# One head per numerator matmul: 64x64 tiles of TensorE in an attention-and-GLU kernel

## The chip, the cores and the metric

The kernel runs on one core of one Trainium2 chip. The metric is the device time of one execution in microseconds (us); where several executions were timed, their median. The changed kernel is compared with the kernel before on the same inputs.

## The reference, cut to what matters

Four batches of 1088 tokens, four heads of 32 numbers. Each query and key is mapped to 64 features (an outer product of two projections to 8), attention is linear in these features, and the result goes through a gated feed-forward layer (GLU) of width 1536.

```python
q_p, k_p = phi(q), phi(k)                       # [b, h, s, 64]
kv  = einsum('bhsf,bhsd->bhfd', k_p, v)         # 64 x 32 for each batch and head
z   = sum(k_p, over s)                          # 64 for each batch and head
num = einsum('bhsf,bhfd->bhsd', q_p, kv)        # the numerators
den = einsum('bhsf,bhf->bhs', q_p, z) + 1e-6
x   = num / den                                 # [b, s, h*32] = 4352 tokens x 128
xn  = x / sqrt(mean(x*x) + 1e-6) * rms_g
out = (silu(xn @ w_gate) * (xn @ w_val)) @ w_out
```

## The kernel before, in words

**Chunks.** The 4352 query tokens are worked in nine chunks: eight of 512 tokens and a last one of 256. `kside(b)` builds, for each batch, the table `kv` (key features times values, with a column of ones beside the values, so that numerator and denominator come out of one matmul). `qside(c)` builds the query features `phiq` of a chunk, then numerators, division, normalization and the two rounded halves `x_hi` and `x_lo` of the layer's input. `slot(c, j, t)` is one of the 12 blocks of 128 columns of the GLU for one chunk: three matmul passes each into `g_ps` and `v_ps` (L788) and three into `o_ps` (L826). These are called dense passes here.

**Small matmuls.** Beside the dense passes, TensorE runs fp32 matmuls on parts of the array. The trace shows each of them as two MATMUL records with a weight load (LDWEIGHTS) before each, so 16 matmuls of the program are 32 records. The forms that matter (rows of the array by columns of the array, as the trace writes them): L505 and L580 128*64 (projections of the first batch and of the first two chunks), L517 (`kvmm`: `kv`) 128*64 in batch 0 and 128*32 in the others, L483 and L608 64*32 (projections), L664 (`nmm`: the numerators) 128*64 in chunks 0 and 1 and 128*32 from chunk 2 on. L588 and L744 are transposes with the whole array.

**The numerators.** Heads are held in pairs `p`: `phiq[:, p, :]` has the 64 features of one head in partitions 0 to 63 and of the other in 64 to 127, and `kv[:, p, :]` is block-diagonal, so that a matmul over 128 rows gives both heads in 66 columns; half of what it multiplies is zeros. From chunk 2 (`spread`, L646) a matmul takes 32 tokens; a task `nmm` covers two blocks of 128 tokens with 16 matmuls and writes one PSUM bank (`att`, of which there are three, `ATT`). Behind it: `den` (add epsilon; ACT or DVE), `rden` (reciprocal, DVE), `x` (multiply, DVE, L672), two `mean` (L695, DVE), then for the chunk `rstd` (POOL, L707), `xn` (DVE or ACT), and from chunk 2 on a turn through DRAM (`xq`, `turned`, `xt`).

**What sets the order.** Each piece of work is a task of a planner (`Plan`). `ORDER` is a list of task numbers written into the file, `ON` a string that says on which engine a task runs that may run on several. Every engine executes its tasks in the order of that list; the planner's own costs (`pe(490, ...)` and the like) only place warm-up matmuls. DMAs of weights, keys, values and queries stand in the same list, on SP's queue.

**Instruction counts.** All dense passes count one MATMUL record each. The 2238 records of TensorE come in the order that the list sets.

Of the kernel before, what the change touches and what calls it, by code (L numbers as in the profile page):

```python
# [86 lines left out]
"""  # L87
ON = (
    "dapapadaddaadaadddaaaaapapdapapaadaadaadaapaadaadaadaadaddaadppddaapaadaaddadadadadadadadpdddaadddaaapapadadapapaadapapd"
    "dapapadapadapdpddddpadaaddadaapadaddpddadddadapadapddddadpadaadapaddpadapadddapapddadaaadpdaadpadadapddadddddapdpddddddd"  # L90
    "ddaaaapapapddapapdpdpddadaddpadadddaaaddddpapddadaddpadddapaddaddddaaddddpddapadadapadaddddpadpadddadadadadddapdda"
# [195 lines left out]
def attention_then_glu(ctx, tc, kT, v, qT, sw, w, out):  # L287
# [13 lines left out]
    def gate(i):  # L301
        return ps(("g_ps", "v_ps")[i], 2)
# [255 lines left out]
    def qside(c):  # L558
# [86 lines left out]
        x, xn = sb("x", [P, 4, H, D], 2), sb("xn", [P, 4 * DM], 2)  # L645
# [3 lines left out]

        def scaled_of(lo, hi):  # L650
            return xn()[:, :nt * DM].rearrange("p (h t d) -> p t h d" if spread else "p (t h d) -> p t h d", h=H, t=nt)[:, lo:hi]

        for u in range(0, nt, 2):
            num = gate(u // 2 if NUM_GATE < 2 else 1) if c <= NUM_GATE else ps("att", ATT)
            den, rden = sb("den", [P, 8, 1], 2), sb("rden", [P, 8, 1], 2)
            wide = D if spread else HALF

            def nmm(u=u, num=num, wide=wide):
                nv = num()[:, :4 * 66].rearrange("p (t a x) -> p t a x", t=2, a=2)
                for t in range(2):  # L660
                    for p in range(2):
                        for n0 in range(0, P, wide):
                            l0 = n0 // D * g + (u + t) * D if spread else (u + t) * P + n0
                            nc.tensor.matmul(  # L664
                                out=nv[n0:n0 + wide, t, p, :], lhsT=phi()[:, p, l0:l0 + wide], rhs=kvs[(s0 + l0) // S][:, p, :], start=True, stop=True,
                            )

            def view(num=num):
                return num()[:, :4 * 66].rearrange("p (y x) -> p y x", x=D + 1)

            def divide(u=u, view=view, rden=rden):
                nc.vector.tensor_tensor(  # L672
                    out=x()[:, u:u + 2], in0=view()[:, :, :D].rearrange("p (t h) d -> p t h d", t=2),
                    in1=rden().rearrange("p (t h) o -> p t h o", t=2).to_broadcast([P, 2, H, D]), op=ALU.mult,
                )
# [259 lines left out]
```

## Time and profile before

| | |
|---|---|
| median of 3 runs | 253.28 us (252.86, 253.28, 255.46) |
| the profiled execution: its time, its span | 252.8 us, 250.6 us |
| TensorE busy | 245.6 us, 98% of the span |
| VectorE, ScalarE, GpSimd busy | 180.4, 132.9, 82.1 us (72, 53, 33%) |
| chain that ended last, share of TensorE | 96% |
| first dense pass starts; last one starts | 16.18 us; 246.44 us |

The span is the profiled execution from its first to its last instruction; the time of that execution is 2.2 us longer. A busy TensorE is not at its peak: records of small matmuls lie over one another, so starts, not durations, tell how fast they pass.

### The profile page before, as it was taken

How to read it: one execution, taken by the hardware profiler on the slowest of the kernel's cores; microseconds unless marked ns; L12 is line 12 of the kernel's file. 1: busy time of each engine (PE TensorE's matmuls, PEld its weight loads, DVE VectorE, ACT ScalarE, POOL GpSimd, SP SyncE). 2: the span in 40 equal slices, each digit the busy share in tenths (PEclk: the TensorE clock that was granted, in tenths of full speed). 3: DMA queues.
4: the chain of work that ended last, by engine and by line, in shares of the span. 5: the costliest groups of instructions: out<-in, count | busy, mean ns of one | idle time of the engine just before them, and what ended most of it. 6: DMA issues, size and time to landing. Idle time of an engine off the chain costs nothing.

```text
span 250.6 us, 5851 instructions
## 1 busy us (share of the span) xinstructions
PE 245.6 (98%) x2238; PEld 197.8 (79%) x2238; DVE 180.4 (72%) x410; ACT 132.9 (53%) x287; POOL 82.1 (33%) x80
## 2 busy tenths in 40 slices
PE   7999999998999999999999999999999999999995
PEld 4977788776888788888888788888888888888894
DVE  1999989798367887675587678855678576765672
ACT  3696987574344747353445643553356464355351
POOL 4547130442663223223450403265332203132201
PEclk9999999999999999999999999999999999999999
DMA  6989992642372332421610352250003001010010
GB/s 235 368 274 347 271 244 77 166 143 44 74 213 67 85 83 94 105 86 32 163 55 1 60 165 86 42 177 35 3 0 63 24 3 42 28 56 3 0 43 21
DMA packets 18539, 25.55 MB, mean 102 GB/s; under 512 B 3024, under 2 KB 9296, under 8 KB 18512
## 3 DMA queue, kind: packets, MB, share of 16 engines
q1 hardware_dynamic: 18080, 24.54, 33.3%
q10 hardware_dynamic: 432, 0.66, 0.7%
q8 instruction: 17, 0.28, 0.5%
q14 instruction: 10, 0.08, 0.1%
HBM read 20.40 MB, written 4.78 MB: 100 GB/s over the span
## 4 chain that ended last, share of the span: by engine, by line
PE 96%; DMA 1%; issue 0%; SPq 0%; DVE 0%
PE v_ps L788 29%; PE g_ps L788 29%; PE o_ps L826 28%; PE att L664 3%; PE att L517 2%; DMA q<-qT 1%; PE att L608 1%; PE o_ps L517 1%; PE att L744 1%; PE att L483 1%; PE g_ps L664 0%; PE att L588 0%; PE v_ps L664 0%; PE att L580 0%; PE att L807 0%
## 5 line engine op out<-in xcount | busy, mean ns | idle before, releaser
L797 ACT ACTIVATE s<-g_ps 128x512 f32<-128x512 f32 (+1 forms) x108 | 61.1, 574 | 71.4 <-PE g_ps L788 38.5
L800 DVE TENSOR_TENSOR h<-v_ps,s 128x512 f32<-128x512 f32 (+2 forms) x110 | 69.7, 646 | 40.0 <-PE v_ps L788 27.6
L818 POOL TENSOR_TENSOR h_lo<-h,h_hi 128x512 fp32r<-128x512 f32 (+1 forms) x42 | 53.0, 1269 | 105.0 <-DVE h_lo L818 43.8
L339 ACT CAST h_hi<-h 128x512 fp32r<-128x512 f32 (+1 forms) x70 | 41.3, 601 | 19.9 <-DVE h L800 17.5
L818 DVE TENSOR_TENSOR h_lo<-h,h_hi 128x512 fp32r<-128x512 f32 (+1 forms) x64 | 41.3, 651 | 5.5 <-ACT h_hi L339 3.6
L788 PE MATMUL v_ps<-x_hi,w_hi 128*128 128x512 f32 (+1 forms) x110 | 41.9, 381 | 0.0
L788 PE MATMUL g_ps<-x_hi,w_hi 128*128 128x512 f32 (+1 forms) x110 | 41.8, 380 | 0.0
L788 PE MATMUL v_ps<-x_hi,w_lo 128*128 128x512 f32 (+1 forms) x110 | 41.6, 378 | 0.0
L788 PE MATMUL g_ps<-x_hi,w_lo 128*128 128x512 f32 (+1 forms) x110 | 41.6, 378 | 0.0
L788 PE MATMUL g_ps<-x_lo,w_hi 128*128 128x512 f32 (+1 forms) x110 | 41.5, 378 | 0.0
L788 PE MATMUL v_ps<-x_lo,w_hi 128*128 128x512 f32 (+1 forms) x110 | 41.3, 378 | 0.0
L826 PE MATMUL o_ps<-h_hi,w_hi 128*128 128x512 f32 (+1 forms) x106 | 40.9, 386 | 0.0
L826 PE MATMUL o_ps<-h_hi,w_lo 128*128 128x512 f32 (+1 forms) x106 | 40.8, 385 | 0.0
L826 PE MATMUL o_ps<-h_lo,w_hi 128*128 128x512 f32 (+1 forms) x106 | 40.8, 385 | 0.0
L788 PEld LDWEIGHTS v_ps<-x_hi,w_hi 128*128 128x128 f32 x110 | 20.6, 188 | 5.0 <-DVE w_lo L422 0.5
L788 PEld LDWEIGHTS g_ps<-x_hi,w_hi 128*128 128x128 f32 x110 | 20.7, 188 | 4.5
L788 PEld LDWEIGHTS v_ps<-x_hi,w_lo 128*128 128x128 f32 x110 | 20.7, 188 | 4.3
L788 PEld LDWEIGHTS g_ps<-x_hi,w_lo 128*128 128x128 f32 x110 | 20.7, 188 | 4.2
L788 PEld LDWEIGHTS g_ps<-x_lo,w_hi 128*128 128x128 f32 x110 | 20.6, 188 | 4.1
L788 PEld LDWEIGHTS v_ps<-x_lo,w_hi 128*128 128x128 f32 x110 | 20.5, 188 | 4.2
L826 PEld LDWEIGHTS o_ps<-h_lo,w_hi 128*128 128x128 f32 x106 | 19.9, 188 | 4.3
L826 PEld LDWEIGHTS o_ps<-h_hi,w_hi 128*128 128x128 f32 x106 | 19.9, 188 | 4.2
(110 smaller groups left out, 245.0 us busy)
## 6 DMA issues: line engine op xcount, KB each, us to landing
w_raw<-w SPq DMA_DIRECT2D x12, 384.0 KB
bt<-far SPq DMA_DIRECT2D x24, 128.0 KB
at<-far SPq DMA_DIRECT2D x12, 256.0 KB
outT<-o_sb SPq DMA_DIRECT2D x8, 256.0 KB
q<-qT SPq DMA_DIRECT2D x7, 256.0 KB
turned<-xq SPq DMA_DIRECT2D x24, 64.0 KB
xt<-turned SPq DMA_DIRECT2D x6, 256.0 KB
vt<-v SPq DMA_DIRECT2D x4, 272.0 KB
```

The source lines that it names most:

```text
L339: "act": on_act(n, lambda: nc.scalar.copy(out=out(), in_=in_()), True),
L483: nc.tensor.matmul(out=pair[p]()[a * D:(a + 1) * D, :g], lhsT=sblk[p * HALF:(p + 1) * HALF, p * NB // 2:(p + 1) * NB // 2], rhs=kt()[p * H ...
L517: nc.tensor.matmul(out=kvv[r0:r0 + wide, h // 2, :], lhsT=phi()[:, t, h * F + f:h * F + f + wide], rhs=vt()[:, t, h, :], start=(t == 0 and ...
L608: nc.tensor.matmul(out=accs[p]()[a * D:(a + 1) * D, :m], lhsT=sab[rows, p].rearrange("p c o r -> p (c o r)"), rhs=q()[rows, a * m:(a + 1) ...
L664: nc.tensor.matmul(out=nv[n0:n0 + wide, t, p, :], lhsT=phi()[:, p, l0:l0 + wide], rhs=kvs[(s0 + l0) // S][:, p, :], start=True, stop=True,)
L744: nc.tensor.transpose(out=xt()[:, t * P:(t + 1) * P], in_=xn()[:, t * DM:(t + 1) * DM], identity=ident)
L788: nc.tensor.matmul(out=acc()[:, cs], lhsT=wt[:, j, i3, :], rhs=x()[:, cs], start=(i == 0), stop=(i == 2))
L797: act(n, lambda: nc.scalar.activation(out=s()[:, :n], in_=gps()[:, :n], func=AF.Silu), cols(gps, whole[0]), [s])
L800: cs.stop - cs.start, lambda cs=cs: nc.vector.tensor_tensor(out=h()[:, cs], in0=vps()[:, cs], in1=s()[:, cs], op=ALU.mult),
L818: eng.tensor_tensor(out=h_lo()[:, :n], in0=h()[:, :n], in1=h_hi().bitcast(F32)[:, :n], op=ALU.subtract)
L826: nc.tensor.matmul(out=o_ps()[:, :n], lhsT=wt[:, j, 2, :], rhs=x()[:, :n], start=first and i == 0, stop=last and i == 2,)
```

## The change

From chunk 2 on, one numerator task covers the whole chunk. A matmul takes one head: 64 rows (that head's features), 64 tokens as columns of the array, and 33 moving columns instead of 66. The heads in partitions 0 to 63 write one bank, those in 64 to 127 a second. A full chunk has 32 such matmuls, as many as the two tasks before had together. Denominators, reciprocals and divisions are taken for each bank (two of each in a full chunk, as before; in the last chunk of 256 tokens two where one was), and all means of a chunk wait for both divisions. `x` is laid out head by head as `xn` was. Tokens of a chunk stay in natural order through `nmm`; the 32x32 transposes later leave them permuted, which the host undoes on the output's rows. `ORDER` and `ON` are new throughout. The core of the diff:

```diff
-            wide = D if spread else HALF
-            def nmm(u=u, num=num, wide=wide):
...
-                for t in range(2):
-                    for p in range(2):
-                        for n0 in range(0, P, wide):
-                            l0 = n0 // D * g + (u + t) * D if spread else (u + t) * P + n0
-                            nc.tensor.matmul(
-                                out=nv[n0:n0 + wide, t, p, :], lhsT=phi()[:, p, l0:l0 + wide], rhs=kvs[(s0 + l0) // S][:, p, :], start=True, stop=True,
...
-            pe(490, 8 * P // wide, nmm, of + [...], [num], None, 32 if spread else 64)
+        if spread:
+            nums = [ps("att", ATT) for _ in range(2)]
+            def nmm():
+                for t in range(nt):
                     for p in range(2):
+                        for hh in range(2):
+                            rows = slice(hh * F, (hh + 1) * F)
+                            for n0 in range(0, P, HALF):
+                                l0, y = t * P + n0, p * nt + t
+                                nc.tensor.matmul(
+                                    out=nums[hh]()[n0:n0 + HALF, y * (D + 1):(y + 1) * (D + 1)], lhsT=phi()[rows, p, l0:l0 + HALF],
+                                    rhs=kvs[(s0 + l0) // S][rows, p, hh * (D + 1):(hh + 1) * (D + 1)], start=True, stop=True,
+                                )
+            pe(122 * nt + 15, 16 * nt, nmm, [(phi, "p", p) for p in range(2)] + batches(0, n), nums, None, 33)
+            for hh in range(2):
...
+                rden = denominators(nums[hh], view, 2 * nt)
...
+                dve(64 * nt, divide, [nums[hh], rden], [(x, hh)])
+            made_of = {t: [(x, 0), (x, 1)] for t in range(nt)}
...
+        rows = o[s0:s0 + n]
+        res[s0:s0 + n] = rows.reshape(4, n // P, D, DM).transpose(1, 0, 2, 3).reshape(n, DM) if c >= XT else rows
```

How the new list moves TensorE's instructions is shown at three places. A row is one kind of instruction: line, output and inputs (with running numbers), output partitions x columns, and how often it comes in a row.

TensorE before, from the projection of a chunk (L608) over the `kv` products of batch 2 (L517) to the two numerator tasks of chunk 3:

```order
L608 MATMUL att_1107<-q_949,sab 32x128 x4
L608 MATMUL att_1112<-q_949,sab 32x128 x4
L517 MATMUL att_1118<-vt_589,phi_987 32x34 x72
L664 MATMUL att_1204<-kv_75,phiq_1105 32x66 x16
L664 MATMUL att_1228<-kv_75,phiq_1105 32x66 x16
```

The same products of batch 2 in the change, with L483 (keys' projection) ahead and one numerator task behind (here L682; 16 rows like the last two, in alternation):

```order
L483 MATMUL att_1119<-kt_984,sblk 32x288 x4
L483 MATMUL att_1124<-kt_984,sblk 32x288 x4
L517 MATMUL att_1131<-vt_580,phi_931 32x34 x72
L682 MATMUL att_1215<-kv_75,phiq_1103 64x33 x2
L682 MATMUL att_1218<-kv_75,phiq_1103 64x33 x2
```

L517 and the numerators had the same form of 128*32 and now have different ones; the projection of queries (L608), which stood in this group, now stands alone among dense passes. Over the whole program, from the first dense pass on, the small fp32 matmuls stood in 9 places among the dense passes and now stand in 12; the three numerator tasks that stood last in one place of 48 matmuls (chunks 7 and 8) now stand in two places, of 32 and 16.

TensorE before, around the first numerators of the program (L664 on 128*64, chunk 0):

```order
L517 MATMUL o_ps_210<-vt_114,phi_142 64x34
L517 MATMUL att_211<-vt_114,phi_142 64x34
L588 MATMUL att_262<-ident,at_217 128x128 x4
L664 MATMUL g_ps_271<-kv_73,phiq_208 64x66 x8
L664 MATMUL v_ps_284<-kv_73,phiq_208 64x66 x8
L588 MATMUL att_298<-ident,at_217 128x128 x4
```

And now (L713 are these numerators):

```order
L517 MATMUL o_ps_178<-vt_112,phi_143 64x34
L517 MATMUL att_179<-vt_112,phi_143 64x34
L580 MATMUL att_244<-sblk,q_127 64x64 x4
L580 MATMUL att_250<-sblk,q_127 64x64 x4
L713 MATMUL g_ps_259<-kv_73,phiq_215 64x66 x8
L713 MATMUL v_ps_274<-kv_73,phiq_215 64x66 x8
L588 MATMUL att_290<-ident,at_272 128x128 x4
```

Chunk 1's projection (L580) has come to stand right before the first numerators, and four of its transposes (L588) have gone behind them.

TensorE before, where the dense passes (L788) begin, with the transposes of chunk 0's x (L744) ahead and a warm-up matmul (L369) between them:

```order
L744 MATMUL att_402<-ident,xn_359 128x128 x2
L369 MATMUL att_409<-const-float32-0.0 1x128
L744 MATMUL att_417<-ident,xn_359 128x128 x2
L788 MATMUL v_ps_422<-x_hi_413,w_hi 128x256
L788 MATMUL v_ps_422<-x_hi_413,w_lo 128x256
```

And now (L786 are the transposes, L830 the dense passes):

```order
L786 MATMUL att_377<-ident,xn_352 128x128 x2
L483 MATMUL g_ps_385<-kt_154,sblk 32x288 x4
L483 MATMUL v_ps_390<-kt_154,sblk 32x288 x4
L608 MATMUL att_406<-q_270,sab 32x128 x4
L608 MATMUL att_411<-q_270,sab 32x128 x4
L830 MATMUL g_ps_418<-x_hi_398,w_hi 128x256
L830 MATMUL g_ps_418<-x_hi_398,w_lo 128x256
L786 MATMUL att_427<-ident,xn_352 128x128 x2
L830 MATMUL v_ps_434<-x_hi_398,w_hi 128x256
```

The second pair of transposes now comes after two dense passes, and two projections stand between the first pair and these passes.

## Rows read from the trace of the kernel before

**Rows 1.** By stretch: its length, PE, PEld, DVE, ACT, POOL busy, clock, DMA, GB/s.

```profile
0.00:16.20 16.20, 14.79 (x289) 10.81 (x289) 10.47 (x36) 9.87 (x32) 8.54 (x21) 1.00 0.83 295
62.00:64.00 2.00, 1.60 (x95) 1.50 (x95) 1.04 (x3) 0.72 (x2) 1.20 (x1) 1.00 0.10 22
64.00:120.00 56.00, 56.00 (x526) 44.93 (x526) 39.54 (x87) 28.19 (x56) 19.54 (x17) 1.00 0.34 93
176.00:246.70 70.70, 70.70 (x356) 59.29 (x355) 48.09 (x107) 33.67 (x71) 16.64 (x14) 1.00 0.09 23
```

**Rows 2.** The chain that ended last: start, length, what. A run of dense passes.

```profile
101.99 3.50 PE o_ps L826 x15
```

**Rows 3.** PE's timeline: start, duration, instruction, count. Chunk 2's numerators alone.

```profile
44.51 0.39 PE L788 MATMUL g_ps<-x_lo,w_hi 128*128 128x512 f32 x1
44.83 1.14 PE L664 MATMUL att<-kv,phiq 128*32 128x66 f32 x64
45.90 0.50 PE L826 MATMUL o_ps<-h_hi,w_hi 128*128 128x512 f32 x1
46.23 0.39 PE L826 MATMUL o_ps<-h_hi,w_lo 128*128 128x512 f32 x1
```

**Rows 4.** PE's timeline: a query projection, then numerators.

```profile
83.19 0.39 PE L826 MATMUL o_ps<-h_lo,w_hi 128*128 128x512 f32 x1
83.51 0.45 PE L608 MATMUL att<-q,sab 64*32 64x128 f32 x16
83.89 1.17 PE L664 MATMUL att<-kv,phiq 128*32 128x66 f32 x64
84.98 0.50 PE L788 MATMUL g_ps<-x_hi,w_hi 128*128 128x512 f32 x1
```

**Rows 5.** PE's timeline: projection, kv products and numerators in one place.

```profile
112.80 0.39 PE L788 MATMUL v_ps<-x_lo,w_hi 128*128 128x512 f32 x1
113.50 1.00 PE L517 MATMUL att<-vt,phi 128*32 128x34 f32 x94
114.31 0.23 PE L664 MATMUL att<-kv,phiq 128*32 128x66 f32 x1
115.79 0.51 PE L788 MATMUL v_ps<-x_hi,w_hi 128*128 128x512 f32 x1
```

**Rows 6.** PE's timeline: the same instructions 53 us earlier, with an idle time.

```profile
59.89 0.39 PE L788 MATMUL v_ps<-x_lo,w_hi 128*128 128x512 f32 x1
62.40 0.42 PE L517 MATMUL att<-vt,phi 128*32 128x34 f32 x28 [0.63 <-issue]
63.74 0.49 PE L788 MATMUL g_ps<-x_hi,w_hi 128*128 128x512 f32 x1
```

**Rows 7.** PE's timeline: 128*64 products of batch 0, 34 moving columns.

```profile
8.37 0.22 PE L517 MATMUL o_ps<-vt,phi 128*64 128x34 f32 x1
...
8.49 0.22 PE L517 MATMUL o_ps<-vt,phi 128*64 128x34 f32 x1
```

**Rows 8.** PE's timeline: 128*64 numerators of chunk 0, 66 moving columns.

```profile
11.04 0.69 PE L664 MATMUL g_ps<-kv,phiq 128*64 128x66 f32 x16
11.56 0.64 PE L664 MATMUL v_ps<-kv,phiq 128*64 128x66 f32 x16
12.13 0.33 PE L588 MATMUL att<-ident,at 128*128 128x128 f32 x1
```

**Rows 9.** Weight loads by form: busy us, mean ns | idle before.

```profile
L664 PEld LDWEIGHTS att<-kv,phiq 128*32 128x32 f32 x416 | 6.4, 110 | 1.0 <-issue 0.9
L517 PEld LDWEIGHTS o_ps<-vt,phi 128*64 128x64 f32 x36 | 2.2, 138 | 0.2 <-POOL phi L438 0.2
L608 PEld LDWEIGHTS att<-q,sab 64*32 64x32 f32 x112 | 1.3, 104 | 2.1 <-issue 1.6 <-PE o_ps L826 0.4
```

**Rows 10.** Timelines of PE and ACT at the start.

```profile
10.46 0.66 PE L588 MATMUL att<-ident,at 128*128 128x128 f32 x4
16.18 0.39 PE L788 MATMUL v_ps<-x_hi,w_hi 128*128 128x256 f32 x1
15.07 0.69 ACT L717 ACTIVATE xn<-x,rstd 128x128 f32<-128x128 f32 x2
```

More of the change, by code (lines that the diff above doesn't have):

```diff
@@ L648, in qside, with tokens, x_of @@
         xs[c] = (x_hi, x_lo)
+        def tokens(t, lo, hi):
+            return t()[:, :nt * DM].rearrange("p (h t d) -> p t h d" if spread else "p (t h d) -> p t h d", h=H, t=nt)[:, lo:hi]
+        def x_of(lo, hi):
+            return tokens(x, lo, hi)
         def scaled_of(lo, hi):
-            return xn()[:, :nt * DM].rearrange("p (h t d) -> p t h d" if spread else "p (t h d) -> p t h d", h=H, t=nt)[:, lo:hi]
-        for u in range(0, nt, 2):
-            num = gate(u // 2 if NUM_GATE < 2 else 1) if c <= NUM_GATE else ps("att", ATT)
+            return tokens(xn, lo, hi)
@@ L655, in qside, with batches, denominators @@
+        def batches(lo, hi):
+            return [("kv", b, i) for b in sorted({(s0 + lo) // S, (s0 + hi - 1) // S}) for i in range(2)]
+        def denominators(num, view, wide):
             den, rden = sb("den", [P, 8, 1], 2), sb("rden", [P, 8, 1], 2)
-            wide = D if spread else HALF
-            def nmm(u=u, num=num, wide=wide):
-                nv = num()[:, :4 * 66].rearrange("p (t a x) -> p t a x", t=2, a=2)
-                for t in range(2):
-                    for p in range(2):
-                        for n0 in range(0, P, wide):
-                            l0 = n0 // D * g + (u + t) * D if spread else (u + t) * P + n0
-                            nc.tensor.matmul(
-                                out=nv[n0:n0 + wide, t, p, :], lhsT=phi()[:, p, l0:l0 + wide], rhs=kvs[(s0 + l0) // S][:, p, :], start=True, stop=True,
-                            )
@@ L668, in view @@
[L668 to L674, printed above, removed]
-                )
-            if spread:
-                bs = {(s0 + a * g + (u + t) * D) // S for a in range(4) for t in range(2)}
-            else:
-                bs = {(s0 + (u * P)) // S, (s0 + (u + 2) * P - 1) // S}
@@ L681, in qside @@
-            of = [(phi, u)] if c < NATURAL else [(phi, "p", p) for p in range(2)]
-            pe(490, 8 * P // wide, nmm, of + [("kv", b, i) for b in sorted(bs) for i in range(2)], [num], None, 32 if spread else 64)
-            plan.add({
-                "dve": on_dve(20, lambda view=view, den=den: nc.vector.tensor_scalar_add(den(), view()[:, :, D:D + 1], EPS)),
-                "act": on_act(20, lambda view=view, den=den: nc.scalar.activation(
-                    out=den(), in_=view()[:, :, D:D + 1], func=AF.Copy, bias=EPS), against=DEN_ACT),
-            }, [num], [den])
@@ L688, in qside @@
-            dve(45, lambda den=den, rden=rden: nc.vector.reciprocal(out=rden(), in_=den()), [den], [rden])
-            dve(256, divide, [num, rden], [(x, u)])
-            for t in range(2):
-                sq = sb("sq", [P, DM], 2)
-                def mean(t=t, u=u, sq=sq):
-                    one = x()[:, u + t]
-                    nc.vector.tensor_tensor_reduce(
-                        out=sq().rearrange("p (h d) -> p h d", h=H), in0=one, in1=one, scale=1.0 / DM, scalar=EPS, op0=ALU.mult, op1=ALU.add,
-                        accum_out=ms()[:, u + t:u + t + 1],
-                    )
-                plan.add({"dve": Way(265, 345, mean, True)}, [(x, u)], [sq, (ms, u + t)])
+            plan.add({
+                "dve": on_dve(20, lambda: nc.vector.tensor_scalar_add(den()[:, :wide], view()[:, :, D:D + 1], EPS)),
+                "act": on_act(20, lambda: nc.scalar.activation(
+                    out=den()[:, :wide], in_=view()[:, :, D:D + 1], func=AF.Copy, bias=EPS), against=DEN_ACT),
+            }, [num], [den])
@@ new lines, in denominators, with view, divide, nmm @@
+            dve(45, lambda: nc.vector.reciprocal(out=rden()[:, :wide], in_=den()[:, :wide]), [den], [rden])
+            return rden
+        if spread:
+            nums = [ps("att", ATT) for _ in range(2)]
+            def nmm():
+                for t in range(nt):
+                    for p in range(2):
+                        for hh in range(2):
[8 more added lines that the diff above has]
+            for hh in range(2):
+                def view(hh=hh):
+                    return nums[hh]()[:, :2 * nt * (D + 1)].rearrange("p (y x) -> p y x", x=D + 1)
+                rden = denominators(nums[hh], view, 2 * nt)
+                def divide(hh=hh, view=view, rden=rden):
+                    nc.vector.tensor_tensor(
+                        out=x()[:, :nt * DM].rearrange("p (a r t d) -> p r a t d", a=2, r=2, t=nt)[:, hh],
+                        in0=view()[:, :, :D].rearrange("p (a t) d -> p a t d", a=2),
+                        in1=rden()[:, :2 * nt].rearrange("p (a t) o -> p a t o", a=2).to_broadcast([P, 2, nt, D]), op=ALU.mult,
+                    )
+                dve(64 * nt, divide, [nums[hh], rden], [(x, hh)])
+            made_of = {t: [(x, 0), (x, 1)] for t in range(nt)}
+        else:
+            for u in range(0, nt, 2):
+                num = gate(u // 2 if NUM_GATE < 2 else 1) if c <= NUM_GATE else ps("att", ATT)
+                def nmm(u=u, num=num):
+                    nv = num()[:, :4 * 66].rearrange("p (t a x) -> p t a x", t=2, a=2)
+                    for t in range(2):
+                        for p in range(2):
+                            for n0 in range(0, P, HALF):
+                                l0 = (u + t) * P + n0
+                                nc.tensor.matmul(
+                                    out=nv[n0:n0 + HALF, t, p, :], lhsT=phi()[:, p, l0:l0 + HALF], rhs=kvs[(s0 + l0) // S][:, p, :],
+                                    start=True, stop=True,
+                                )
+                def view(num=num):
+                    return num()[:, :4 * 66].rearrange("p (y x) -> p y x", x=D + 1)
+                pe(490, 16, nmm, [(phi, u)] + batches(u * P, (u + 2) * P), [num], None, 64)
+                rden = denominators(num, view, 8)
+                def divide(u=u, view=view, rden=rden):
+                    nc.vector.tensor_tensor(
+                        out=x_of(u, u + 2), in0=view()[:, :, :D].rearrange("p (t h) d -> p t h d", t=2),
+                        in1=rden().rearrange("p (t h) o -> p t h o", t=2).to_broadcast([P, 2, H, D]), op=ALU.mult,
+                    )
+                dve(256, divide, [num, rden], [(x, u)])
+            made_of = {t: [(x, t // 2 * 2)] for t in range(nt)}
@@ L702, in qside, with mean @@
+        for t in range(nt):
+            sq = sb("sq", [P, DM], 2)
+            def mean(t=t, sq=sq):
+                one = x_of(t, t + 1)[:, 0]
+                nc.vector.tensor_tensor_reduce(
+                    out=sq().rearrange("p (h d) -> p h d", h=H), in0=one, in1=one, scale=1.0 / DM, scalar=EPS, op0=ALU.mult, op1=ALU.add,
+                    accum_out=ms()[:, t:t + 1],
+                )
+            plan.add({"dve": Way(265, 345, mean, True)}, made_of[t], [sq, (ms, t)])
         for u, wd in ((0, 2), (2, 2)) if first else ((0, nt),):
@@ L703, in qside @@
             us, cs = slice(u, u + wd), slice(u * P, (u + wd) * P)
-            ids = list(range(u, u + wd, 2))
+            ids = sorted({k for t in range(u, u + wd) for k in made_of[t]}, key=lambda k: k[1])
             def root(us=us):
@@ L710, in scaled @@
                 nc.vector.tensor_tensor(
[L711 removed]
+                    out=scaled_of(u, u + wd), in0=x_of(u, u + wd),
                     in1=rstd()[:, u:u + wd].unsqueeze(3).to_broadcast([P, wd, H, D]), op=ALU.mult,
@@ L722, in qside @@
                 "act": Way(wd * 300 + 5, wd * 300 + 85, scaled_act, against=SCALED_ACT),
-            }, [(x, i) for i in ids] + [(rstd, u)], [(xn, u)])
+            }, ids + [(rstd, u)], [(xn, u)])
             if spread:
@@ L933 @@
     r = run_bass_kernel_spmd(nc, [arrays], core_ids=[0])
-    return np.ascontiguousarray(r.results[0]["outT"].T)
+    o = r.results[0]["outT"].T
+    res = np.empty((NT, DM), np.float32)
+    for c, (s0, n) in enumerate(zip(STARTS, CHUNKS)):
+        rows = o[s0:s0 + n]
+        res[s0:s0 + n] = rows.reshape(4, n // P, D, DM).transpose(1, 0, 2, 3).reshape(n, DM) if c >= XT else rows
+    return res
```

11 lines of the change are left out of this document (5 added, 6 removed), and 70 rows, old and new, of the table ORDER.

## The prediction

> **What bounds the kernel now.** I read the busy time by stretch first. TensorE is busy for 56.00 of 56.00 us and for 70.70 of 70.70 us in the stretches after 64 us, while the next busiest engine, DVE, has 39.54 and 48.09 [rows 1]. So TensorE is the bound, and the kernel's end moves by what its instruction stream gains or loses. The chain of waits then tells what a dense pass costs: 15 passes of 512 columns in 3.50 us, so 0.233 us each [rows 2]. Before and after each group of small matmuls the timeline gives the rest: from the start of the last dense pass before the group to the start of the second one after it, less two passes of 0.233, is what the group costs. The chunk's numerators alone cost 46.23 - 44.51 - 0.47 = 1.25 us [rows 3]. Only the start (up to 16.18 us [rows 10]) and a hole near 62 us, where TensorE is busy for 1.60 of 2.00 us [rows 1], are not full.
>
> The sum below is made against the profiled execution, 252.8 us with a span of 250.6; it lies 0.5 under the median of the three runs, 253.28, and nothing in the change touches the 2.2 us outside the span.
>
> **The numerators themselves.** A full chunk keeps its 32 matmuls, hence 64 records with 64 weight loads, and six full chunks and a half one have them (6.5 in full chunks). Before, four tiles of 128*32 work side by side: 64 records pass in 45.90 - 44.83 = 1.07 us [rows 3], or 16 rounds of four records; taking off an estimated 0.13 for the first load and the last record's way out leaves 59 ns a round. Now a round is again four records, on four tiles of 64*64, and each tile streams 33 columns instead of 66. What does a round cost when the columns are halved? Three rows bound it.
>
> - The same tile of 128*64 takes a new record every 0.06 us with 34 moving columns: 8.37 and 8.49 with one between [rows 7]. With 66 columns its 32 records take 12.13 - 11.04 = 1.09 us [rows 8], which is 16 rounds of two tiles, again 0.06 a round once 0.13 is taken off. Half the columns, the same time: there the moving columns don't bind, and what is left is the weight load, whose 64 columns both have in common. Its recorded length is 138 ns for 64 columns and 110 for 32 [rows 9]; with 64 rows instead of 128 at 32 columns it is 104 against 110, so fewer rows hardly shorten it.
> - The 128*32 tiles with 34 columns pass 94 records in 114.31 - 113.50 = 0.81 us, 8.6 ns each, 34 ns a round [rows 5]. Here the loads have 32 columns.
> - With 128*64, two tiles side by side give 29 ns a record (the 0.058 to 0.06 of rows 7 over two).
>
> The changed matmul has 64 columns to load and 33 to stream, like rows 7 in both, but four tiles instead of two. I take it that the two halves of the rows load beside each other: 58 ns a round, 16 rounds, 0.93 us against 0.94 before. That gains 0.02 in a chunk, **-0.1 us in all**. The lower end is the rate of the 32-column loads: 16 x 34 = 0.55, 0.39 less in a chunk, -2.5 us. The upper end is that the halves of the rows must load one after the other: 16 x 117 = 1.87, 0.93 more, +6.0 us. I take the value nearest to rows 7, since these share both sizes with the new matmul.
>
> The Trainium skill ("TensorE: Matmul & The Clock Gate", LDWEIGHTS) says that a load takes its number of columns over 1.2 GHz whatever the rows, which for 64 columns would be an estimated 53 ns; no run here shows 64*64 yet. The Trainium skill ("TensorEngine Tiling (Array Packing)", Instruction Overhead) warns not to cut a dimension that is already small, because a matmul of one moving column takes as long as one of 60: by that, 66 to 33 columns would be worth only a tenth of a round, an estimated 0.6 us in all. The trace disagrees in one form: the 34-column records of rows 5 pass in rounds of 34 ns, the 66-column ones in 59.
>
> **Where the groups stand.** Dense passes have 128*128, so a group pays on entering and leaving: its first record starts 44.83 - 44.51 = 0.32 after the last dense pass, 0.09 more than a pass, and the second dense pass behind it starts 46.23 - 45.90 = 0.33 after the first, 0.10 more [rows 3]. So a group that stands alone costs 0.19 more than one that follows another small group of a different form: 83.89 to 84.98 is 1.09 for the numerators behind L608, again close to 1.07 [rows 3, 4]. From the first dense pass on there were 9 places with small fp32 matmuls and there are now 12: 3 x 0.19 = **+0.6 us**. Behind L517 the numerators had the same form and paid nothing for a change. The place of rows 5 costs 116.13 - 112.80 - 0.47 = 2.86 (its second dense pass starts 0.34 after 115.79), that of L608 with L517 alone would be an estimated 2.0 (0.41 for L608, by which rows 4 exceed rows 3; 144 records of 8.6 ns, 1.24; 0.32 for entering, leaving and the last record's way out); so the numerators add 0.87 there, against 1.09 behind a different form. Two places before have L517 and numerators together, and in the change both have a change of form between them: 2 x 0.22 = **+0.4 us**.
>
> **The hole at 62 us.** The same 224 records take 63.74 - 59.89 = 3.85 us in rows 6 and 115.79 - 112.80 = 2.99 in rows 5. The 0.86 between them is a time in which TensorE had nothing to run and no semaphore to wait for; the row names the issue of instructions [rows 6]. It falls behind 114 records of 8.6 ns each, in a place of 224, and doesn't in the other place of 224; so whether such a place runs dry depends on where it falls in the stream. The change has again two places of 224 records (L483 or L608, L517, L682). The ends are no hole, -0.86, and two, +0.86. I count half a hole, **-0.4 us**, since one in two fell before.
>
> **The start.** The order up to the first dense pass is new. Out of the path to the first numerators go four transposes, 11.04 - 10.46 = 0.58 us [rows 8, 10]; in their place stand the projections of chunk 1, 16 records on 128*64, 0.5 by the rate of rows 7, while the copies of kv that the numerators need would have to be waited for anyway. Against that the second pair of transposes of x now stands behind only two dense passes of 128x256 (0.23 us together: 256 columns, so half of 0.233 each), and the scaling that it needs takes 0.69 on ACT [rows 10], now behind `x_hi`. I take **0**, with -0.6 (the transposes' 0.58) and +0.6 (0.69 less what those two passes cover) as ends. SP's queue loads chunk 1's queries later, behind two weights and values; what waits for that is L580, which moved back as well.
>
> **What costs nothing.** DVE and ACT do the same denominators, reciprocals and divisions of 128x8 and 128x256 in a full chunk; the last chunk has one set more. The strided reads of the means could lengthen them, and all four now wait for both divisions. DVE stands idle for 16.46 of 56.00 us in [rows 1], and TensorE has several microseconds of dense passes between a chunk's numerators and its use, so neither shows; without that cover the longer wait would be one division and two means on DVE per chunk.
>
> **Sum.** -0.1 + 0.6 + 0.4 - 0.4 + 0 = +0.5 us, so 252.8 + 0.5 = 253.3 us. Within 1% of the median, 2.5 us, counts as no change, which is about what a measurement of this kernel can tell.
>
> **The rivals.** (1) *The columns do bind.* If the loads of 64 rows hide or are shorter, the round falls to 34 ns and the numerators give -2.5: 252.8 - 2.5 + 0.6 + 0.4 - 0.4 = 250.9. For it speaks that 128*32 with 34 columns passes at 8.6 ns a record [rows 5]; against it, that 128*64 does not get there with the same 34 columns [rows 7]. (2) *The halves of the rows share one way to load.* Then a round is two loads, 117 ns, and the kernel is slower: 252.8 + 6.0 + 0.6 + 0.4 - 0.4 = 259.4. It begins to cost when a round is over 59 ns; over 1% slower, 255.8, is 2.4 us more than the other terms leave (253.4), which over 6.5 x 16 = 104 rounds is 23 ns, so from a round of 82 ns. For it: no row shows 64-column loads in both halves; L608 runs on 64*32, but its 128 moving columns cover any load (16 records in 0.38 us, [rows 4]). Against it: rows 9 give no sign that rows matter, and the halves have partitions of their own. (3) *The new order fails at the start or at a full place:* both places of 224 run dry (+0.9 instead of -0.4) and the start loses 0.6: 252.8 - 0.1 + 1.0 + 0.9 + 0.6 = 255.2. For it speaks that these depend on arrivals which one trace before cannot show; against it, that nothing stalled in the other stretches of rows 1. (4) *The start gains its 0.6* and no place runs dry: 252.8 - 0.1 + 1.0 - 0.9 - 0.6 = 252.2, still no change.
>
> **How the numbers follow.** Forecast, rival (4) among it: 0.63. Rival (1) 0.20, rival (2) 0.08, rival (3) 0.09. The range takes in (1) with a little of a better start, 250.6, and (3), 255.2; only (2) and the far ends of the others are left out. The likeliest case alone reaches from 252.2 to 254.6. Faster by over 1% (under 250.75) needs (1) with a better start, 0.09 with a little for an order that gains more than I see; slower by over 1% (over 255.8) is (2) and the far part of (3), 0.12; the rest, 0.79, is within 1%.
>
> **What would show it.** In the timeline after: 64 records of L682 alone among dense passes take about 1.05 us from their start to that of the first dense pass (0.67 by rival 1, 2.0 by rival 2). The second dense pass behind each group is 0.33 after the first, at 12 places. Idle time of PE with the releaser "issue" tells the holes. The first dense pass starts near 15.7 to 16.2 us, with the second pair of transposes behind it. Wrong would be: DVE or POOL named as what TensorE waits for after 17 us, or a granted clock under 1.00 [rows 1] in a full stretch.

## The result, and the profile after

The changed kernel takes 255.52 us (median of 17 runs, 254.12 to 255.92 with one disturbed at 271.07), the kernel before in the same rounds 253.36 (17 runs). The ratio, of the means of all but the disturbed run, is 1.0062, with a 95% interval of 1.0037 to 1.0087: slower by more than the measurement is uncertain, and inside the 1% that counted as no change. The forecast of 253.3 had the class right and the time wrong: 255.5 lies 0.3 above the range.

The profiled execution took 255.82 us, with a span of 253.7. First the windows again, as in [rows 1] (stretch: its length, then busy time of PE, PEld, DVE, ACT, POOL, clock, DMA, GB/s):

```profile
0.00:18.10 18.10, 16.68 (x285) 12.79 (x285) 9.82 (x33) 10.24 (x30) 8.94 (x22) 1.00 0.81 289
64.00:120.00 56.00, 56.00 (x724) 44.80 (x710) 42.85 (x101) 25.88 (x53) 18.23 (x14) 1.00 0.38 95
176.00:248.90 72.90, 72.90 (x392) 60.62 (x391) 42.89 (x96) 37.04 (x78) 30.41 (x27) 1.00 0.08 22
```

TensorE is full in both long stretches again, so the end still moves by what its stream gains or loses. The first row is the news: the start is 18.1 us long, where it was 16.2.

The new numerators alone, in PE's timeline of the changed kernel (start, duration, instruction, count), to set beside [rows 3]:

```profile
50.25 0.40 PE L868 MATMUL o_ps<-h_lo,w_hi 128*128 128x512 f32 x1
50.58 1.14 PE L682 MATMUL att<-kv,phiq 64*64 64x33 f32 x64
51.64 0.50 PE L830 MATMUL v_ps<-x_hi,w_hi 128*128 128x512 f32 x1
51.98 0.40 PE L830 MATMUL v_ps<-x_hi,w_lo 128*128 128x512 f32 x1
```

From 50.58 to 51.64 is 1.06 us, where 44.83 to 45.90 was 1.07, and the place costs 51.98 - 50.25 - 0.47 = 1.26 (1.25 before). Record by record the start advances 117 ns per eight, so 58.4 ns a round of four. The weight loads, of after (busy us, mean ns | idle), answer to [rows 9]:

```profile
L682 PEld LDWEIGHTS att<-kv,phiq 64*64 64x64 f32 x416 | 6.7, 134 | 1.9 <-issue 1.5 <-DVE h L842 0.4
L517 PEld LDWEIGHTS att<-vt,phi 128*64 128x64 f32 x36 | 2.5, 148 | 0.0
```

A place of 224 records of the changed kernel, for [rows 5] and [rows 6]:

```profile
62.71 0.40 PE L830 MATMUL v_ps<-x_lo,w_hi 128*128 128x512 f32 x1
63.04 0.71 PE L483 MATMUL att<-kt,sblk 64*32 64x288 f32 x16
63.69 1.44 PE L517 MATMUL att<-vt,phi 128*32 128x34 f32 x144
65.05 1.14 PE L682 MATMUL att<-kv,phiq 64*64 64x33 f32 x64
66.12 0.50 PE L830 MATMUL v_ps<-x_hi,w_hi 128*128 128x512 f32 x1
```

There is no idle time in it, nor in the other place of 224.

Now the start. Four transposes of L588 and the first dense pass, before (for [rows 10]), then after:

```profile
7.21 0.66 PE L588 MATMUL g_ps<-ident,at 128*128 128x128 f32 x4
7.70 0.60 PE L588 MATMUL v_ps<-ident,at 128*128 128x128 f32 x4
...
246.57 1.05 PE L807 MATMUL att<-h,w_f 128*128 128x128 f32 x8
```

```profile
8.18 1.12 PE L588 MATMUL g_ps<-ident,at 128*128 128x128 f32 x4
9.09 1.05 PE L588 MATMUL v_ps<-ident,at 128*128 128x128 f32 x4
...
18.07 0.38 PE L830 MATMUL g_ps<-x_hi,w_hi 128*128 128x256 f32 x1
...
249.22 1.06 PE L849 MATMUL att<-h,w_f 128*128 128x128 f32 x8
```

The same four transposes take 0.49 us from start to start before and 0.91 after. That is TensorE's two levels, 2.4 and 1.2 GHz: by the trace's record of the granted clock it rose at 4.36 us in the execution before and at 10.01 in the one after. The clock column of a windows view, 1.00 in both first rows, doesn't show it; the pace of an unchanged instruction does. The last line of each fence is the last group of matmuls. With it the 3.1 us of span divide: first dense pass later, 18.07 - 16.18 = +1.89; from there to the last group, 231.15 against 230.39, +0.76; from there to the end of the span, 4.47 against 4.06, +0.41.

So two questions were open: is the late rise of the clock the change's doing, and what are the 0.76 and 0.41?

### The profile page after: what moved, and what is told of

Same layout as the page of the kernel before. It is cut to its first block, busy times and chain, and to the rows that moved or that the text cites. A ratio compares the mean times of both kernels' runs of the same rounds, so it can differ in the third digit from the quotient of the medians.

```text
span 253.7 us, 5844 instructions
## 1 busy us (share of the span) xinstructions
PE 248.8 (98%) x2236; PEld 200.1 (79%) x2236; DVE 175.6 (69%) x397; ACT 133.6 (53%) x286; POOL 91.8 (36%) x91
## 4 chain that ended last, share of the span: by engine, by line
PE 94%; DMA 1%; DVE 1%; ACT 1%; SPq 0%; issue 0%; DVEq 0%
PE g_ps L830 29%; PE v_ps L830 28%; PE o_ps L868 28%; PE att L682 3%; PE att L517 2%; DMA q<-qT 1%; PE o_ps L517 1%; PE att L608 1%; PE att L483 1%; ACT xn L759 1%; PE v_ps L505 0%; PE g_ps L588 0%; PE att L580 0%; PE att L849 0%; PE att L786 0%; PE v_ps L588 0%
## 5 line engine op out<-in xcount | busy, mean ns | idle before, releaser
L860 POOL TENSOR_TENSOR h_lo<-h,h_hi 128x512 fp32r<-128x512 f32 (+1 forms) x50 | 61.0, 1230 | 97.0 <-DVE h_lo L860 32.8
L339 ACT CAST h_hi<-h 128x512 fp32r<-128x512 f32 (+1 forms) x73 | 43.4, 603 | 15.5 <-DVE h L842 11.8
L860 DVE TENSOR_TENSOR h_lo<-h,h_hi 128x512 fp32r<-128x512 f32 (+1 forms) x56 | 36.6, 666 | 8.6 <-POOL h_lo L860 6.2
L830 PE MATMUL g_ps<-x_hi,w_hi 128*128 128x512 f32 (+1 forms) x110 | 42.5, 386 | 0.0
L830 PE MATMUL v_ps<-x_hi,w_hi 128*128 128x512 f32 (+1 forms) x110 | 41.9, 381 | 0.0
L830 PE MATMUL v_ps<-x_hi,w_lo 128*128 128x512 f32 (+1 forms) x110 | 41.7, 379 | 0.0
L830 PE MATMUL g_ps<-x_hi,w_lo 128*128 128x512 f32 (+1 forms) x110 | 41.7, 379 | 0.0
L830 PE MATMUL v_ps<-x_lo,w_hi 128*128 128x512 f32 (+1 forms) x110 | 41.6, 379 | 0.0
L830 PE MATMUL g_ps<-x_lo,w_hi 128*128 128x512 f32 (+1 forms) x110 | 41.5, 378 | 0.0
L830 PEld LDWEIGHTS g_ps<-x_hi,w_hi 128*128 128x128 f32 x110 | 20.6, 188 | 4.9 <-issue 0.4
L830 PEld LDWEIGHTS v_ps<-x_hi,w_hi 128*128 128x128 f32 x110 | 20.6, 188 | 4.8 <-DVE h L842 0.3
L830 PEld LDWEIGHTS v_ps<-x_lo,w_hi 128*128 128x128 f32 x110 | 20.7, 188 | 4.7 <-issue 0.5
L830 PEld LDWEIGHTS g_ps<-x_lo,w_hi 128*128 128x128 f32 x110 | 20.7, 188 | 4.2
L830 PEld LDWEIGHTS v_ps<-x_hi,w_lo 128*128 128x128 f32 x110 | 20.7, 188 | 4.2
L830 PEld LDWEIGHTS g_ps<-x_hi,w_lo 128*128 128x128 f32 x110 | 20.7, 188 | 3.9
```

The lines of the kernel that those rows point to most:

```text
L339: "act": on_act(n, lambda: nc.scalar.copy(out=out(), in_=in_()), True),
L830: nc.tensor.matmul(out=acc()[:, cs], lhsT=wt[:, j, i3, :], rhs=x()[:, cs], start=(i == 0), stop=(i == 2))
L860: eng.tensor_tensor(out=h_lo()[:, :n], in0=h()[:, :n], in1=h_hi().bitcast(F32)[:, :n], op=ALU.subtract)
```

## The experiments

**New tiles in the old order, and old tiles in the new order.** The first gives the numerators their new form and leaves the tasks where they stood (one numerator task stands where the second of a pair stood, the last chunk's three dense passes later for want of a bank); the second keeps the 128x32 matmuls and takes the new sequence. Only the order's table and the form differ:

```diff
 e1_tiles_only: form of the change;  ORDER, ON: those of the kernel before, carried over task by task
 e2_order_only: form of the kernel before;  ORDER, ON: those of the change, carried over task by task
```

> The new numerators in the old order (one numerator task stands where the second of a pair stood; the last chunk's stands three dense passes later, for want of a PSUM bank). Theory: the tiles themselves cost nothing, the new order does. So the start is the old one (first dense pass near 16.2 us), 64 records take about 1.05 us, the hole of 0.86 near 62 us stays, two changes of form and one place more cost 0.7, and a wait behind L608, whose pair of banks must be free before the numerators get two, some tenths: about 254 us, ratio to before 1.002 to 1.005. Rival: the tiles cost what the change lost; then the ratio is 1.006 to 1.01 with this order as well.

> The old numerators (128*32, 66 columns) in the new order, two tasks where one stood. Theory: the loss lies in the order, at its start and in its 12 places of small matmuls. So it keeps nearly all of it: first dense pass near 18.1 us if the clock rises at 10 us as in the changed kernel's trace, and 0.4 less than the change where numerators follow L517 in the same form: ratio to before 1.004 to 1.006. Rival: the tiles cost it; then the ratio is within 1.000 to 1.002.

Tiles only: 257.55 us, ratio 1.0140 (1.0097 to 1.0183), more than either expectation. Order only: 254.92 us, 1.0044 (1.0012 to 1.0076). The form by itself loses, and the order gives most of that back. Where it loses, in PE's timeline of tiles only:

```profile
85.32 0.39 PE L868 MATMUL o_ps<-h_lo,w_hi 128*128 128x512 f32 x1
85.64 0.45 PE L608 MATMUL att<-q,sab 64*32 64x128 f32 x16
86.02 0.60 PE L369 MATMUL att<-const-float32-0.0 128*1 128x128 f32 x4
86.68 1.14 PE L682 MATMUL att<-kv,phiq 64*64 64x33 f32 x64
87.75 0.50 PE L830 MATMUL g_ps<-x_hi,w_hi 128*128 128x512 f32 x1
```

Four warm-up records of zeros (L369) stand between the query projection and the numerators: the planner's fill for a wait. There are three `att` banks, L608 holds two of them, and the new numerators want two at once. The place costs 2.30 us by the measure of [rows 4] (1.67 there); the same happens near 141 us, and the last chunk, short of a bank, needs one more place of 1.11 us. That is what the new order is for, and why it has more places: it moves numerators out from behind L608. Its own price against the same order with the old tiles is small: the numerators behind L517 cost 0.13 more in each of the two places of 224 records (3.28 against 3.14, 3.01 against 2.88), alone the same (1.26 both).

**The start: filling the gaps, and the old start.** One kernel puts two warm-up matmuls into the gaps at 4.5 to 5.8 us, the other takes the old sequence up to the first dense pass.

```diff
 e3_fill
+FILL = {32: 1, 37: 1}
-            if e == "pe" and at - clock[e] > GAP:
-                k = int((at - clock[e] - SPARE) / UNIT)
+            if e == "pe" and (at - clock[e] > GAP or i in FILL):
+                k = FILL.get(i, int((at - clock[e] - SPARE) / UNIT))
 e4_old_start
 ORDER: tasks of the old start up to the first dense pass first, then the rest of the change's order
```

> The changed kernel with two warm-up matmuls more, in the gaps of TensorE before and between the first two query projections (4.5 to 5.4 us). Theory: the start is late since TensorE runs at the lower of its two clock levels until 10.0 us, where before it rose at 4.4 us; with the gaps filled it rises earlier, the first dense pass starts at 16.2 to 16.8 us and the time falls by 1.3 to 1.9 us: ratio to before 1.000 to 1.003. Rival: the new order's start is late by its chain of waits; then nothing changes, first dense pass at 18 us or later, ratio 1.006 to 1.009.

> The changed kernel with the old order (and engines) up to the first dense pass, the new order from there. Both theories of the late start expect a gain: if the clock by chance rises late, the first dense pass is late here as well (over 17.5 us) and the ratio stays at 1.006 or more, which would speak for the clock as such; if the clock rises at 4 to 7 us, the first dense pass starts at 16.2 to 16.8 and the ratio is 1.000 to 1.004. If the start is at 16.2 to 16.8 with a late clock, the clock is not the cause.

Both missed. The fill took 255.43 us (1.0088, 1.0054 to 1.0123), and its clock rose at 9.34 us in the one execution traced. As 3 of its 7 runs lie between 254.4 and 254.8, that doesn't show whether those gaps matter. The old start took 257.64 us (1.0188, 1.0148 to 1.0228). It does not fit what follows: twenty warm-up records stand between its first dense passes,

```profile
20.69 1.05 PE L369 MATMUL att<-const-float32-0.0 128*1 128x128 f32 x8
...
22.10 1.49 PE L369 MATMUL att<-const-float32-0.0 128*1 128x128 f32 x12
```

so it says nothing about the start. Its clock showed something else: it rose at 3.49 us, fell at 6.90, after TensorE had waited 1.4 us for a query load, and rose again at 10.31.

**Both kernels once more.** If the clock's rise is not the change's doing, either kernel has early and late executions. The two kernels were run unchanged.

> The kernel before, unchanged, for a second trace. Theory: the time of its start hangs on when TensorE's clock rises, which varies from run to run (4.4 us in the first trace; 8.6 in a run with the same start). If it rises at 4 to 5 us, the first dense pass starts near 16.2 and the span is about 250.6; if it rises at 8 to 10 us, near 18 and 252.5. Rival: the start is 16.2 us whatever the clock does.

> The changed kernel, unchanged, for a second trace. Theory: with a clock that rises before 6 us the first dense pass starts at 16.2 to 16.6 and the span is 251.7 to 252.3, about 1.2 over that of the kernel before with an early clock (the places of small matmuls, less the hole, and the transposes that moved); with a late one 18.0 and 253.5. Rival: 18 us with an early clock as well.

They came out the other way round. The kernel before took 254.82 us, with the late clock (rise at 9.87 us):

```profile
8.63 1.12 PE L588 MATMUL g_ps<-ident,at 128*128 128x128 f32 x4
9.54 0.76 PE L588 MATMUL v_ps<-ident,at 128*128 128x128 f32 x4
...
18.19 0.39 PE L788 MATMUL v_ps<-x_hi,w_hi 128*128 128x256 f32 x1
...
248.61 1.05 PE L807 MATMUL att<-h,w_f 128*128 128x128 f32 x8
```

The changed kernel took 254.13 us, with the early one (5.01 us):

```profile
7.08 0.66 PE L588 MATMUL g_ps<-ident,at 128*128 128x128 f32 x4
7.79 0.66 PE L588 MATMUL v_ps<-ident,at 128*128 128x128 f32 x4
...
16.43 0.39 PE L830 MATMUL g_ps<-x_hi,w_hi 128*128 128x256 f32 x1
...
247.53 1.06 PE L849 MATMUL att<-h,w_f 128*128 128x128 f32 x8
```

Now like can be compared with like:

| | run, us | first dense pass | to the last group | to the end |
|---|---|---|---|---|
| before, early | 252.80 | 16.18 | 230.39 | 4.06 |
| after, early | 254.13 | 16.43 | 231.10 | 4.47 |
| before, late | 254.82 | 18.19 | 230.42 | 4.06 |
| after, late | 255.82 | 18.07 | 231.15 | 4.47 |

The late clock costs either kernel 1.7 to 2.0 us, all of it ahead of the first dense pass. Two kernels further down that keep the start of the kernel before agree: clock at 3.71 us and first dense pass at 16.27 (split), 9.18 and 17.85 (shift). The change costs +1.3 us between the early ones and +1.0 between the late ones; its start is worth +0.25 and -0.12, so nothing that two pairs could settle. The 1.1 us behind the first dense pass are in both. Each row is one execution. By the runs, the kernel before has a median of 253.2 below 254 us (40 runs) and 255.0 above (41), the changed kernel 254.3 (two runs) and 255.6 (14), so +1.1 and +0.5.

**What sets the round.** Each of two kernels changes one size of the new matmul: 60 moving columns for 33, and weight tiles of 64x32 for 64x64, which doubles the records. (With 60 columns, what reads the result skips the 27 that belong to the other head; that part is left out here.)

```diff
 e5_wide
-    out=nums[hh]()[n0:n0 + HALF, y * (D + 1):(y + 1) * (D + 1)], rhs=...[rows, p, hh * (D + 1):(hh + 1) * (D + 1)]
+    out=nums[hh]()[n0:n0 + HALF, y * 60:(y + 1) * 60], rhs=...[rows, p, hh * 6:hh * 6 + 60]
 e6_short_loads
-    for n0 in range(0, P, HALF):  ... lhsT=phi()[rows, p, l0:l0 + HALF]
+    for n0 in range(0, P, D):     ... lhsT=phi()[rows, p, l0:l0 + D]
```

> The changed kernel with 60 moving columns instead of 33 in each numerator matmul of 64*64 (27 of them belong to the other head and are not read). Theory: the weight load of 64 columns sets the round, so 64 records alone among dense passes still take 1.07 us from the first start to the next dense pass. If the moving columns set it, the round of 58 ns grows to about 106 and the place takes 1.8 us.

> The changed kernel with 32 tokens as the array's columns (64*32, eight tiles, 64 matmuls and 128 records in a chunk). Theory: a load of 32 columns takes half as long, so a record's pace is no longer 14.6 ns but that of L517's 32-column records, 8.4 ns: 128 records take 1.1 to 1.2 us, no better than 64 at 14.6. If a record has a pace of its own whatever its load, 128 take 1.9 us.

With 60 columns (254.57 us in one execution, early clock), then with short loads:

```profile
49.20 1.16 PE L682 MATMUL att<-kv,phiq 64*64 64x60 f32 x64
50.29 0.49 PE L830 MATMUL v_ps<-x_hi,w_hi 128*128 128x512 f32 x1
```

```profile
63.31 0.58 PE L517 MATMUL att<-vt,phi 128*32 128x34 f32 x46
63.82 0.43 PE L682 MATMUL att<-kv,phiq 64*32 64x33 f32 x33
68.10 1.01 PE L682 MATMUL att<-kv,phiq 64*32 64x33 f32 x95 [3.86 <-issue]
69.05 0.61 PE L830 MATMUL v_ps<-x_hi,w_hi 128*128 128x512 f32 x1
69.45 0.63 PE L830 MATMUL v_ps<-x_hi,w_lo 128*128 128x512 f32 x1
69.88 0.63 PE L830 MATMUL v_ps<-x_lo,w_hi 128*128 128x512 f32 x1
```

Nearly twice the columns pass in 1.09 us instead of 1.06, still 117 ns per eight records; half the loaded columns pass at 67 ns per eight. So the load of 64 columns sets the round, not the columns streamed; nor its rows, since rounds of 128*64 take the same 58 to 60 ns [rows 7]. (A tile's width and its load's columns are one size, so these two can't be told apart here.) The Trainium skill ("TensorE: Matmul & The Clock Gate", LDWEIGHTS) has the load depend on its columns alone, an estimated 53 ns for 64 and 27 for 32; the rounds of 58.4 and 33.4 ns agree within 7 ns. The short loads cost 264.93 us all the same: with 288 records in a place TensorE stood 3.86 us with nothing to run, the clock fell behind that, and dense passes took 0.43 us until it was back; a second hole, of 2.48 us at 118 us, did the same.

**A start without gaps.** 16 warm-up records at the very start for 12, none by the planner before the first scores, two in each gap before the queries; in either kernel.

```diff
-WARM, WARM_COLS = 6, 128
+WARM, WARM_COLS = 8, 128
+FILL = {14: 0, 32: 1, 37: 1}
 (and the two lines of the planner as above)
```

> The changed kernel with TensorE kept at work in its first 5.5 us: 16 warm-up records of 128 columns at the start in place of 12, none by the planner before the first scores, and two each in the two gaps before the query blocks (4.4 and 5.1 us), so that the three idle stretches of 0.3 to 0.5 us between 3.1 and 5.4 us shrink. Open is why the changed kernel's executions have the late clock (first dense pass at 18.1 us, 255.2 to 255.9 us) far more often than the kernel before. Theory A (the idle stretches ahead of the rise decide whether it comes early): the granted clock rises before 7 us, the first dense pass starts at 16.2 to 16.6 us, and most runs lie at 254.0 to 254.5 us. Theory B (the phase of the clock's steps against the start decides, not the idle time): most runs stay at 255.2 to 256.2 us, the first dense pass of the profile at about 18.

> The kernel before with the same fill of the first 5.5 us. Theory A: nearly all runs at 252.7 to 253.3 us, none at 254.8 to 255.5, where about a quarter of the kernel's runs lay so far. Theory B: the shares stay as they were, three quarters low, a quarter near 255; both are raised by up to 0.4 us if the longer warm-up pushes the first scores back.

The kernel before so filled took 252.98 us (12 runs, 252.48 to 253.73), ratio **0.9952** (0.9926 to 0.9978): its median is below that of both kernels. Its clock rose at 5.66 us, and none of its twelve runs lies above 253.8, where 19 of the 29 of the kernel before in these rounds lay above 254. It is no faster than the low runs of the kernel before (252.6 to 253.9): its first dense pass starts at 17.04 us, 0.86 behind the early execution and 1.15 ahead of the late one. What is missing is the high group. In the changed kernel the rise came at 5.98 us, but the first dense pass only at 17.38, and the 12 runs spread from 254.45 to 256.63 (median 255.30, 1.0041, 1.0013 to 1.0069): theory A's numbers missed there. Part of the gain of the kernel before so filled is something else, in its place near 61 us:

```profile
61.17 0.45 PE L609 MATMUL att<-q,sab 64*32 64x128 f32 x16
61.55 1.44 PE L518 MATMUL att<-vt,phi 128*32 128x34 f32 x144
62.91 1.14 PE L665 MATMUL att<-kv,phiq 128*32 128x66 f32 x64
63.97 0.50 PE L789 MATMUL g_ps<-x_hi,w_hi 128*128 128x512 f32 x1
```

The hole of [rows 6] is gone, 0.73 us by the whole place (2.99 against 3.72).

**The hole.** Two kernels asked what it belongs to, both made from the kernel before: one moves the third chunk's numerators behind the next task of three dense passes, the other puts six warm-up records in front of an earlier place.

```diff
 f1_split_burst
-676 438 236 238 678 240 677 443 923 449 396 349 350 356 361 241 277 342 362 397
+676 438 236 238 678 240 677 923 396 349 350 356 361 241 277 342 362 443 449 397
 h1_shift
+FILL = {552: 3}    (and the two lines of the planner as above)
```

> The kernel before with the 64 numerator matmuls of the third chunk moved one dense pass later, out of the place of 224 records near 60 us into a place of their own. If the hole of 0.86 us there belongs to the length of the burst: L608+L517 cost 1.9 to 2.0 us and the numerators alone 1.25, together 3.2 in place of 3.7, first dense pass to last matmul 230.6 us in place of 231.2, and the median 252.7 to 253.0, about 0.2% under the kernel before, within what the rounds can tell. If the hole is not of the burst's length it turns up in the other place of 224 records (112.8 us, 2.9 us so far) or in one of the two halves, and the stretch stays at 231.2 or grows to 231.4.

> The kernel before with six more warm-up records (three calls) ahead of the query projection at 26.7 us and nothing else: every later TensorE instruction stands six records further back in the stream, as in the kernel before with the filled start, while the start and the place near 60 us keep their own work and arrivals. In the three traces of the kernel before and of the one with the split burst the idle time labelled issue came behind the same record, the 114th of L517 near 61.8 us. Theory P (it belongs to the position in the instruction stream): the place near 60 us passes its 224 records without it, 2.9 to 3.0 us in place of 3.6 to 3.7, or the idle time moves to another record there; the six records cost 0.65 us and the median moves by under 0.1%. Theory T (it is the timing of that execution, and the filled start escaped it because it began later): it comes again behind the 114th record, 0.5 to 0.9 us long.

The split, then the shift:

```profile
60.60 1.19 PE L517 MATMUL att<-vt,phi 128*32 128x34 f32 x114
62.65 0.45 PE L517 MATMUL att<-vt,phi 128*32 128x34 f32 x30 [0.86 <-issue]
```

```profile
63.50 1.44 PE L518 MATMUL att<-vt,phi 128*32 128x34 f32 x144
64.78 1.14 PE L665 MATMUL att<-kv,phiq 128*32 128x66 f32 x64
65.85 0.49 PE L789 MATMUL g_ps<-x_hi,w_hi 128*128 128x512 f32 x1
```

Splitting didn't help (254.49 us, 0.9997, 0.9961 to 1.0033): the hole came behind the same 114th record of L517, where it also came in the second execution of the kernel before (0.48 us) and in tiles only (0.70). Six records further along it is gone, though that execution had the late clock, like the second one of the kernel before, which showed it. So it hangs on where the burst stands in the instruction stream, and not on its length alone. In the shifted kernel the place at 28 us, whose 144 records took 1.92 us for 1.52, lost 0.4 instead; whether that is the same thing isn't shown (254.58 us, 0.9993, 0.9961 to 1.0026).

The traces say what the holes have in common. Their DMA queue for instructions (q8) brings packets of 16,384 bytes, 17 in these kernels and 21 with short loads. Counting MATMUL and LDWEIGHTS records together, 1729 stand ahead of the hole in all four traces, and 1985 and 3266 ahead of the two holes with short loads: 256 further on, and six times 256 but for one record. In all six the first matmul behind the hole starts 1.30 to 1.46 us after such a packet has landed, and at no place of this count, in any of the traces, does TensorE go on sooner than that. In the changed kernel the 1729th record also stands in a burst, but its packet had landed 2.4 us earlier, and no time was lost. So the instructions came late; why they were fetched late there and not elsewhere wasn't tried. The Trainium skill ("Runtime: NRT & Kernel Launch", Instruction fetch mechanics) has instructions come in blocks, with the crossing mostly hidden; that holds here under dense passes and not in all bursts of small matmuls.

## Why the prediction was right, and where it was not

- **The numerators, -0.1.** Right in mechanism and size: a round of 58.4 ns was measured for the 58 forecast, and rivals 1 and 2, which hung on the round, fell with it, as the two kernels with 60 columns and with short loads show. That the time stayed is a coincidence of sizes: before, with loads of 32 columns, a round took 34 ns with 34 moving columns and 59 with 66 [rows 3, 5], so the moving columns set it; now the load of 64 columns does, and takes as long.
- **Places and form, +0.6 and +0.4.** The form change was mis-sized: 0.13 in each of two places, so 0.26 in place of 0.4. The places, twelve as forecast, cost about 0.7 by the order alone against the kernel before, and the second dense pass comes 0.33 to 0.34 behind the first at eleven of them (at the twelfth transposes stand between). The step left out one: the second pair of transposes of x is a small group too, and stands in the middle of dense passes now, where it costs 0.4 to 0.5 us that lay ahead of the first dense pass before.
- **The hole, -0.4.** That it hangs on the place in the stream was the right thought; the outcome was no hole at all, -0.86.
- These terms, the transposes among them, come to about +0.5 us; measured between the first dense pass and the last group are +0.7 in either pair (four more transposes that now stand apart cost 0.07, a wait near 193 us 0.09), where the forecast, without a start, had +0.5. That the two are so close is luck: the hole and the form came out 0.6 lower than forecast, the places, the transposes and the numerators about as much higher.
- **The start, 0.** This is the step that failed. The forecast priced what tasks stand in the start, and there the pairs give +0.25 and -0.12, inside its ends. But it read 16.18 us off one execution and took it for the kernel's, although one of the three runs before, 255.46, lay 2.2 us above the next. The clock's rise moves the start by 1.6 to 2.0 us from run to run, and neither the sum nor a rival had that.
- **The end.** 0.4 us more behind the last matmuls in both pairs was in no term. It is in order only too, not in tiles only; between two of SyncE's closing semaphore instructions lie 0.4 us instead of 0.07. What delays them wasn't tried.

Of the 2.2 us between the medians, then, 1.0 to 1.3 are the change by the two pairs, 0.5 to 1.1 by the groups of runs. The rest is which group a median falls into: in those rounds 11 of 17 runs of the kernel before lay under 254, and 14 of the 16 undisturbed ones of the changed kernel above 255. Over all rounds the kernel before was low in 40 of 81 runs. Whether the new order makes the late clock likelier or drew it more often is open: 2 of 16 runs against 11 of 17 were low in the same rounds, but three of four traced executions with this start had the early clock (the second one, 60 columns, short loads: 5.01, 4.60 and 4.44 us). The filled start shows only that what TensorE does ahead of 6 us bears on it in the kernel before.

## What to carry to other kernels

Before cutting the moving columns of small matmuls on tiles, compare the same tile at two widths: where the time doesn't change, the weight load's columns set the round, and only fewer loaded columns help. A row-tiled form that needs two accumulation banks at once costs order, and order costs places. Compare executions of the same clock phase: read when an unchanged instruction reaches its full pace, and look at the runs' spread for two groups before a median is explained.

## What the runs showed of the hardware

- The granted clock rose between 3.5 and 10.0 us in executions whose first 3 us were alike; late, the start took 1.6 to 2.0 us more.
- It also fell: behind 1.4 us of waiting at 5 us, and behind holes of 3.86 and 2.48 us; behind the first, dense passes took 0.43 us each until it rose again.
- A burst of small matmuls can run dry while its instructions are still on their way: 0.5 to 0.9 us behind the 114th record in four traces of three kernels, 3.86 and 2.48 in places of 288 records, each time until 1.30 to 1.46 us after an instruction packet had landed.
- Rounds of records on tiles side by side took 58.4 ns with 64 loaded columns, whether 33 or 60 were streamed, and 33.4 with 32 loaded and 33 streamed.
